# A spectral mixer with MLP: the rests' transposes in another bank pair, the last group's steps at later slots, the plain tiles' copies and stores moved, the last stores on two queues

## The chip, the cores and the metric

The kernel runs on one core of one Trainium2 chip. The metric is the device time of one execution in microseconds, from first to last instruction with what lies around it; lower is better. The core has a matrix engine (TensorE, PE in the profile, with its weight loads as PEld), a vector engine (VectorE, DVE), a scalar engine (ScalarE, ACT), a general engine (GpSimd, POOL) and an engine that only issues transfers (SyncE, SP). Each takes its own instructions strictly in program order and waits on semaphores for the others. PSUM, the memory that matmuls write, has eight banks; the large on-chip memory is SBUF.

## The reference

Four sublayers follow each other, A, B, A, B, each added to its input. x is 2048 tokens by 576 features, in fp32:

```python
def _A_ref(x, ...):            # Fourier mixing
    a = einsum("bsd,ed->bse", x, dft_hid_re)
    b = einsum("bsd,ed->bse", x, dft_hid_im)
    return einsum("ts,bse->bte", dft_seq_re, a) - einsum("ts,bse->bte", dft_seq_im, b)

def _B_ref(x, w1, b1, w2, b2): # MLP, 576 -> 4608 -> 576
    y = _layernorm(x)
    h = _gelu(einsum("bsd,df->bsf", y, w1) + b1)
    return einsum("bsf,fd->bsd", h, w2) + b2

x = x + _A_ref(_layernorm(x), ...)
x = x + _B_ref(_layernorm(x), ...)
x = x + _A_ref(_layernorm(x), ...)
x = x + _B_ref(_layernorm(x), ...)
```

## The kernel before

Every fp32 operand is split into a high and a low part (fp32r), and a product is made of three matmuls: high by high, high by low, low by high (`PASSES`). On top of it, products of 2 by 2 blocks are done with seven block products in place of eight, in the order 1, 6, 2, 5, 7, 3, 4 (`ORDER`). Sums and differences of blocks, the conversions to the high part (ScalarE) and the subtractions that give the low part (VectorE, a few on POOL) are the other engines' work. The order of all instructions is written out by hand, with Python generators that are advanced step by step; nothing is reordered afterwards.

A layer has these stages.

**Sequence** (`Sequence`, `run` at L693) multiplies by the DFT along the tokens. Two output tiles are *plain*: `first_mms` computes them with eight block products while the input is still being prepared by the steps of `fill`, tile 0 into banks 4 to 7 and then tile 1 into banks 0 to 3. `first_post` (L599) copies the four banks of one of them to a block of SBUF with four ScalarE copies, and stores the block to DRAM (`uvd`). The other 14 tiles run group by group, seven groups each: `low` (VectorE) and `high` (ScalarE) prepare the coming groups, `mms` runs 24 matmuls of one group, and `post` reads its bank. Blocks of the DFT matrix come through a ring of six (`load_c`, L622); a block goes back to the ring when `low` has used it for the last time, and the next load follows. Loads and most stores go through `dma`, which is SP's queue. `pump` advances the background work that prepares the MLP's weights.

**Hidden** (`hidden`, L869) multiplies by the DFT along the features, normalizes, and turns the tokens into the layout that the MLP wants, y, with TensorE transposes. Blocks have 288 features, two times 128 and a *rest* of 32; the rests are transposed on their own. For the last pair of tiles `turn_y` (L962) does it, in six steps: four with transposes and splits of the large parts, in bank pairs that `space` hands out, then two with the transposes and ScalarE copies of the rests (L982 to L988). The rests' transposes write the upper halves of banks 0 to 3. They are interleaved with the start of the MLP: each `next(mlp)` runs one group of seven matmuls of the first half of the tokens, whose results stand in the lower halves of the same banks.

**MLP** (`mlp`, L1061) runs on half of the tokens at a time, so four times in all. `inner(q)` (L1164) computes hidden block q, q = 0 to 17 with F = 4608, in seven groups, and leaves eight *steps* in a list: each makes one high part (ScalarE, L1235), one low part (L198, on VectorE or POOL) and perhaps a sum. `outer(g, i, side)` (L1260) multiplies two hidden blocks by the second weights, 12 matmuls per slot, two slots per i, with eight slots on one side and six on the other. `work` runs the next step of the list: once in each group of `inner`, and in two slots of three of `outer`, or in every slot from `g >= last - 1` on. An order of slots and steps that is typical: `inner(2g)`, eight slots of group g-1 (side 1), `inner(2g+1)`, six slots (side 0).

In the very first MLP the second weights are also made: `make` (L1102) returns a list of (slot number, step), and `advance` runs the steps that are due. The last group (g = 8) has a list of its own, at L1129, with its subtractions on VectorE. After a slot VectorE adds the bank to the goal (L1285, a helper at L195), and the next slot but one uses that bank again.

The final tiles are stored by `store` (L1367), in the order 4, 5, 6, 7, 0, 1, 2, 3 of the half.

`Heap` keeps the free stretches of two large SBUF tiles, and `alloc` takes the stretch that has been free the longest.

Of the kernel before, what the change touches and what calls it, by code (L numbers as in the profile page):

```python
# [8 lines left out]
F32 = mybir.dt.float32  # L9
# [148 lines left out]
def spectral_mixer(ctx: ExitStack, tc: tile.TileContext, x, dh, c0, cs, w1, b1, w2, b2, out):  # L158
# [32 lines left out]
    def dma(dst, src):  # L191
        nc.sync.dma_start(dst, src)
# [4 lines left out]
    def sub(engine, dst, a, b):  # L197
        engine.tensor_tensor(dst, a, b, op=OP.subtract)  # L198
# [122 lines left out]
    class Sequence:  # L321
# [277 lines left out]
        def first_post(self, t, out):  # L599
            uv = out(2, 2, DH)  # L600
            for i in range(2):
                for j in range(2):
                    nc.scalar.activation(uv[:, i, 1 - j], banks[4 * (1 - t) + 2 * i + j][:, :DH], AF.Copy,
                                         scale=-1.0 if i else 1.0)
            dma(uvd[t], out(2 * D))


        def load_block(self, t, k, block):
# [84 lines left out]
        def run(self, hidden):  # L693
            for p in range(NP):
                while self.ready <= p:
                    next(self.pieces)
                self.first_mms(p)

            outs = [next(b for b in self.xs if b.at != raw.at)]
            self.xs.remove(outs[0])  # L700
            self.first_post(0, outs[0])
            for _ in self.pieces:
                pass
            if outs[0].at < UV_AT + 4 * D:
                outs.pop().free()
            hidden.reserve()
            steps = self.steps
            outs.append(A.alloc(2 * D))
            self.first_post(1, outs[-1])
            for out in outs:  # L710
                clock[0] += 1
                out.free()
            for n, (t, i) in enumerate(steps):
                self.load_c()
                if n + 2 < len(steps):
                    self.low(*steps[n + 2])
                if i == 2 and t + 1 < NT:
                    self.sums(t + 1)
                self.load_c()
                if n + 3 < len(steps):  # L720
                    self.high(*steps[n + 3])
                self.mms(t, i)
                self.post(t, i)
                if t == NT - 1:
                    hidden.begin(self, ORDER.index(i))
                if n == 3 and not self.early:
                    dma(b1t, b1)
                if n % 3 == 2 and 8 <= n < 8 + 3 * KH and not self.early:
                    dma(dhd[n // 3 - 2], dh[n // 3 - 2])
                if i != 2:  # L730
                    pump()
                    pump()
            for k in range(2):
                self.L[k].free()
            self.own.close()
            for z in self.Z:
                z.free()
            hidden.take()
# [130 lines left out]
    def hidden(h, mlp):  # L869
# [92 lines left out]
        def turn_y(j):  # L962
            v = t8[j](8, DH)
            at = slice(j * P, (j + 1) * P)
            blocks = (1, 3, 2, 4, 5, 6, 7)
            for m, i0 in enumerate((2, 4, 0, 6)):
                if m % 2 == 0:
                    o = space()
                ob = o[:, m % 2]
                ni = min(2, 7 - i0)  # L970
                for i in range(ni):
                    for k in range(2):
                        nc.tensor.transpose(ob[:, (2 * i + k) * P:(2 * i + k + 1) * P],
                                            v[:, blocks[i0 + i], k * P:(k + 1) * P], ident)
                ov = ob[:, :2 * ni * P].rearrange("p (i k t) -> p i k t", k=2, t=P)
                split(y[:, i0:i0 + ni, 0:2, at], y[:, i0:i0 + ni, 3:5, at], ov)
                yield
            for i0 in (0, 4):
                ov = bank[:, i0 // 2:i0 // 2 + 2, 2 * P:].rearrange("p a (b t) -> p a b t", t=P)
                ni = min(4, 7 - i0)  # L980
                for i in range(ni):
                    nc.tensor.transpose(ov[:96, i // 2, i % 2], es(7, 96)[:, blocks[i0 + i] - 1], ident)  # L982
                for i in range(0, ni, 4 if ni == 4 else 2):
                    if ni == 4:
                        nc.scalar.activation(y[:96, 0:4, 2, at].rearrange("p (a b) t -> p a b t", a=2), ov[:96], AF.Copy)
                    else:
                        n = min(2, ni - i)
                        nc.scalar.activation(y[:96, i0 + i:i0 + i + n, 2, at], ov[:96, i // 2, :n], AF.Copy)  # L988
                yield
            t8s.give(t8.pop(j))  # L990

# [47 lines left out]
            next(mlp)  # L1039
        rests(3)  # L1040
        y_steps = turn_y(3)
        for n in (4, 1, 1):
            next(mlp)
            for m in range(n):
                if n == 4 and m == 2:
                    parts(2, slice(0, 4), slice(3, 7), high=False, engine=nc.gpsimd)
                    t8s.give(t8.pop(2))
                next(y_steps)
# [12 lines left out]
    def mlp(hid, store, first, before, after):  # L1061
# [40 lines left out]
        def make(g):  # L1102
            b11, b12, b22, b21, x = (rv[:, k] for k in range(5))
            pool = nc.gpsimd
            other = nc.vector if g == NG - 1 else pool

            def hi(i, src):
                got2[g, i] = c2.take()
                nc.scalar.activation(got2[g, i](2, 2, DH)[:, :, 0], src, AF.Copy)

            def lo(i, src):
                t = got2[g, i](2, 2, DH)
                sub(nc.vector, t[:, :, 1], src, t[:, :, 0].bitcast(F32))
                b = got2[g, i]
                soon(lambda: dma(w2s[g, i - 1], b(2, 2 * DH).bitcast(F32)))

            def soon(step):
                kept.append((at[1] + 2, step))

            one = [lambda: hi(1, b11), lambda: (lo(1, b11), sub(pool, b11, b12, b11), sub(pool, x, b22, b11))]  # L1120
            six = [lambda: hi(6, x), lambda: (lo(6, x), sub(other, x, b21, x))]
            five = [lambda: hi(5, b11), lambda: (lo(5, b11), soon(lambda: load_raw(g + 1, 0)))]
            three = [lambda: hi(3, b22), lambda: (lo(3, b22), sub(other, b12, b22, b12), soon(lambda: load_raw(g + 1, 2)))]
            seven = [lambda: hi(7, b12), lambda: (lo(7, b12), soon(lambda: load_raw(g + 1, 1)))]
            four = [lambda: hi(4, x), lambda: lo(4, x)]
            two = [lambda: hi(2, b21), lambda: (lo(2, b21), soon(lambda: load_raw(g + 1, 3)))]
            if g == NG - 1:
                return (list(zip((24, 25), one)),
                        list(zip((5, 7, 7, 8, 9, 10, 11, 12, 12, 13, 13, 14), six + five + three + seven + four + two)))  # L1129
            return (list(zip((24, 25), one)),  # L1130
                    list(zip((0, 1, 2, 3, 9, 10, 15, 16, 17, 18, 19, 20), five + six + three + seven + four + two)))

# [15 lines left out]
        def work(n):  # L1148
            for _ in range(n):
                if tasks:  # L1150
                    tasks.pop(0)()
# [12 lines left out]
        def inner(q, part=None):  # L1164
# [64 lines left out]
            def step(n):  # L1229
                if n == 0:  # L1230
                    gelu(b[3], b[3], 1)
                if n < 7:
                    k, src = parts[n]
                    H[q, k] = hs.take()
                    nc.scalar.activation(H[q, k](2, TC)[:, 0], src, AF.Copy)  # L1235
                if n:
                    k, src = parts[n - 1]
                    h = H[q, k](2, TC)
                    sub(nc.vector if n < 4 or first and q == NQ - 1 else nc.gpsimd, h[:, 1], src, h[:, 0].bitcast(F32))
                if n == 1:  # L1240
                    add(nc.vector, t, b[1], s3)
                elif n == 2:
                    sub(nc.vector, s3, b[0], s3)
                elif n == 3:
                    sub(nc.vector, s2, t, b[0])
                elif n == 4:
                    sub(nc.vector, u, b[3], s2)
                if n == 7:
                    for b_ in v:
                        tmps.give(b_)  # L1250
                    if q == NQ - 1:
                        tmps.close()
# [7 lines left out]
        def outer(g, i, side):  # L1260
            for jj in range(2):
# [11 lines left out]
                    for f in range(2):  # L1273
                        hs.give(H.pop((2 * g + f, i)))
                clock[0] += 1
                work(slot[0] % 3 < 2 or g >= last - 1)
                slot[0] += 1
                advance()
                if g == last or g == last - 1 and side == 0:
# [80 lines left out]
    for layer in range(2):  # L1360
# [3 lines left out]
        for half in range(2):  # L1364
            here = hid

            def store(j, xv):  # L1367
                t = 8 * half + j
                dma(to[t * P:(t + 1) * P, :].rearrange("p (e d) -> p e d", e=2), xv[:, :, j])

            before = after = iter(())
            if half == 0:
# [52 lines left out]
```

## Time and profile before

| | us |
|---|---|
| median of 3 runs | 2706.81 |
| the runs | 2705.21 to 2708.84 |
| profiled execution | 2707.04 |
| its span, first to last instruction | 2705.2 |
| PE busy | 2669.1 |
| VectorE busy | 1769.2 |
| ScalarE busy | 1101.6 |
| POOL busy | 794.3 |

The granted clock of TensorE was 0.999 of full speed over the span. In the profile's rows a line such as L205 is often that of a helper: L205 is every matmul, L198 every subtraction and L195 every addition on any engine, L192 every transfer on SP's queue. L1174 is a GELU, L1201 the copy of a hidden block's first group, L1235 the high part of a step, L643 the high part of a DFT block, L675 the copy of a tile's first group, L579 the high part of the four sums of an input pair. In a name such as `bank<-R` the tile written stands ahead of the tiles read: A and R are the two large SBUF tiles, bank is PSUM.

### The profile page before, as it was taken

To read this page: it belongs to the slowest core of one execution; us is meant where nothing else is said; L and a number is where in the kernel's file an instruction comes from. 1 tells how busy PE (TensorE), PEld (TensorE's weight loads), DVE (VectorE), ACT (ScalarE), POOL (GpSimd) and SP (SyncE) were. 2 spreads that over 40 slices of the span, in tenths; PEclk is the share of its full clock that TensorE was granted. 3 is DMA by queue.
4 is the path that set the end of the run, shared out by engine and by line. 5 is a ranking of instruction groups with operands and counts; after the bars stand their busy time and mean duration, and the time that the engine had idled before them with its cause. 6 is when DMAs were issued, how large, how long until landed. Compare 5 with 4: busy or idle time off the path is not lost. (4 is left out here: it accounts for less than half of the span.)

```text
span 2705.2 us, 45278 instructions
## 1 busy us (share of the span) xinstructions
PE 2669.1 (99%) x17540; PEld 2500.6 (92%) x17540; DVE 1769.2 (65%) x2573; ACT 1101.6 (41%) x1841; POOL 794.3 (29%) x740
## 2 busy tenths in 40 slices
PE   9999999999999999999999999999999999999998
PEld 9999999888888988998899999998999899898988
DVE  8888866778776565556676666466555546555555
ACT  6555544544443343333354333343333314433331
POOL 6223234544442432222250000142222234322222
PEclk9999999999999999999999999999999999999999
DMA  4777775777777466666454333546666673666664
GB/s 173 264 261 245 242 260 183 262 266 272 263 268 290 151 180 194 195 217 207 153 194 141 124 121 123 192 138 193 194 193 196 190 273 110 208 192 194 192 194 151
DMA packets 209286, 544.92 MB, mean 201 GB/s; under 512 B 22048, under 2 KB 56864, under 8 KB 208928
## 3 DMA queue, kind: packets, MB, share of 16 engines
q1 hardware_dynamic: 197408, 515.48, 58.9%
q10 hardware_dynamic: 11664, 26.55, 2.5%
q8 instruction: 139, 2.28, 0.3%
q14 instruction: 75, 0.61, 0.1%
HBM read 429.87 MB, written 114.72 MB: 201 GB/s over the span
## 5 line engine op out<-in xcount | busy, mean ns | idle before, releaser
L205 PE MATMUL bank<-R 128*128 128x288 f32 (+2 forms) x16972 | 2612.4, 315 | 17.9 <-DVE A L195 9.8
L205 PEld LDWEIGHTS bank<-R 128*128 128x128 f32 x16972 | 2438.6, 189 | 182.0 <-DVE A L195 22.4
L195 DVE TENSOR_TENSOR A<-bank,A 128x576 f32<-128x576 f32 (+3 forms) x808 | 567.9, 709 | 551.2 <-PE bank L205 471.3
L198 POOL TENSOR_TENSOR R<-A,R 128x512 fp32r<-128x512 f32 (+1 forms) x288 | 375.6, 1315 | 913.6 <-ACT R L1235 873.1
L198 DVE TENSOR_TENSOR R<-A,R 128x1024 fp32r<-128x1024 f32 (+9 forms) x521 | 494.5, 972 | 57.2 <-ACT R L643 23.6
L195 POOL TENSOR_TENSOR A<-A 128x576 f32<-128x576 f32 (+2 forms) x102 | 138.0, 1355 | 568.0 <-ACT A L683 365.4
L1174 ACT ACTIVATE bank<-bank,b1t 128x512 f32<-128x512 f32 (+1 forms) x224 | 144.9, 647 | 369.6 <-DVE bank L195 242.7
L1235 ACT ACTIVATE R<-A 128x512 fp32r<-128x512 f32 x288 | 176.0, 628 | 272.4 <-DVE A L198 118.2
L198 POOL TENSOR_TENSOR A<-A 128x384 f32<-128x384 f32 (+3 forms) x156 | 198.2, 1273 | 248.7 <-DVE R L198 128.1
L643 ACT ACTIVATE R<-A 128x1024 fp32r<-128x1024 f32 x196 | 204.6, 1052 | 120.2 <-DVE A L198 97.7
L195 DVE TENSOR_TENSOR bank<-bank,A 128x512 f32<-128x512 f32 (+1 forms) x228 | 152.2, 670 | 144.7 <-PE bank L205 143.8
L198 DVE TENSOR_TENSOR R<-bank,R 128x512 fp32r<-128x512 f32 (+1 forms) x328 | 204.9, 639 | 52.1 <-ACT R L201 46.9
L198 DVE TENSOR_TENSOR A<-A 128x1024 f32<-128x1024 f32 (+3 forms) x134 | 140.9, 1058 | 4.6 <-DVE R L198 0.4
L1201 ACT ACTIVATE A<-bank 128x512 f32<-128x512 f32 (+1 forms) x76 | 43.8, 576 | 234.9 <-PE bank L205 231.4
L1235 ACT ACTIVATE R<-bank 128x512 fp32r<-128x512 f32 x216 | 121.2, 595 | 29.8 <-PE bank L205 29.7
L198 DVE TENSOR_TENSOR A<-bank,A 128x512 f32<-128x512 f32 x144 | 97.9, 680 | 0.0
L201 ACT ACTIVATE R<-bank 128x512 fp32r<-128x512 f32 (+1 forms) x112 | 49.4, 491 | 85.3 <-PE bank L856 79.1
L1174 ACT ACTIVATE A<-bank,b1t 128x512 f32<-128x512 f32 (+1 forms) x76 | 50.6, 666 | 66.0 <-DVE bank L195 66.0
L685 DVE SCALAR_TENSOR_TENSOR A<-A 128x288 f32<-128x288 f32 x28 | 16.0, 572 | 83.3 <-POOL A L195 83.3
L275 ACT ACTIVATE R<-A 128x256 fp32r<-128x256 f32 x126 | 52.0, 413 | 44.3 <-DMA w_parts<-R 18.4
L249 ACT ACTIVATE A<-A,moments 128x576 f32<-128x576 f32 x58 | 48.6, 862 | 48.2 <-POOL moments L230 19.8
L276 ACT ACTIVATE R<-A,power,middle 128x128 fp32r<-128x128 f32 x126 | 60.8, 482 | 0.0
(67 smaller groups left out, 629.2 us busy)
## 6 DMA issues: line engine op xcount, KB each, us to landing
R<-w_parts SPq DMA_DIRECT2D x504, 320.0 KB, 3.4
R<-w_parts SPq DMA_DIRECT2D x189, 576.0 KB, 3.7
A<-in_cs SPq DMA_DIRECT2D x112, 512.0 KB, 4.1
w_parts<-R SPq DMA_DIRECT2D x63, 576.0 KB, 5.1
w_parts<-R ACTq DMA_DIRECT2D x81, 320.0 KB, 3.2
uv_mid<-A SPq DMA_DIRECT2D x32, 576.0 KB, 3.1
w_parts<-R SPq DMA_DIRECT2D x45, 320.0 KB, 4.3
A<-in_w SPq DMA_DIRECT2D x72, 192.0 KB, 4.8
```

The costliest lines, as they stand in the source:

```text
L195: engine.tensor_tensor(dst, a, b, op=op)
L198: engine.tensor_tensor(dst, a, b, op=OP.subtract)
L201: nc.scalar.activation(hi, src, AF.Copy)
L205: nc.tensor.matmul(o, a, b, start=start, stop=stop, skip_group_check=True)
L249: nc.scalar.activation(dst, src, AF.Identity, bias=mv[:, 4:5], scale=mv[:, 3:4])
L275: nc.scalar.activation(t[:, 1:4:2], src[:, 0:3:2], AF.Copy)
L276: nc.scalar.activation(t[:, 2], src[:, 1], AF.Identity, bias=power[:, 2:3], scale=middle)
L643: nc.scalar.activation(self.cells[t, i](2, NP, P)[:, 0], self.source(t, i), AF.Copy)
L685: nc.vector.scalar_tensor_tensor(uv[:, 1, 0], p7, -1.0, u, op0=OP.mult, op1=OP.subtract)
L1174: nc.scalar.activation(dst, src, AF.Gelu_apprx_tanh, bias=bias(f))
L1201: nc.scalar.activation(up, o, AF.Copy)
L1235: nc.scalar.activation(H[q, k](2, TC)[:, 0], src, AF.Copy)
```

## The change

- `turn_y`: the rests' transposes go to a bank pair from `space`, the four of the first step to its first bank, the three of the second step to its second; each step has one ScalarE copy. With (4, 0, 2) in place of (4, 1, 1) both steps come after the MLP's last group of the first token half.
- `run`: the block for the second plain tile is taken from the input ring as well, before the rest of `fill`, in place of a new `alloc` after it; its copies still follow the rest of `fill`. `hidden.reserve()` comes after both blocks are freed. `first_post` stores through ScalarE's queue.
- First MLP: the slots of the last group's list move back by up to two; in block 0, steps 4 and 5 subtract on VectorE instead of POOL.
- All MLPs: in the eight slots of group 7 (`last - 1`), side 1, a step runs in two slots of three.
- Last MLP: tiles with odd j are stored through ScalarE's queue.

```diff
-            dma(uvd[t], out(2 * D))
+            nc.scalar.dma_start(uvd[t], out(2 * D))
...
             self.first_post(0, outs[0])
+            outs.append(next(b for b in self.xs if b.at != raw.at))
+            self.xs.remove(outs[1])
             for _ in self.pieces:
                 pass
-            if outs[0].at < UV_AT + 4 * D:
-                outs.pop().free()
-            hidden.reserve()
-            steps = self.steps
-            outs.append(A.alloc(2 * D))
-            self.first_post(1, outs[-1])
+            self.first_post(1, outs[1])
             for out in outs:
                 clock[0] += 1
                 out.free()
+            hidden.reserve()
+            steps = self.steps
...
+            o = space()
             for i0 in (0, 4):
-                ov = bank[:, i0 // 2:i0 // 2 + 2, 2 * P:].rearrange("p a (b t) -> p a b t", t=P)
+                ov = o[:, i0 // 4].rearrange("p (i t) -> p i t", t=P)
                 ni = min(4, 7 - i0)
                 for i in range(ni):
-                    nc.tensor.transpose(ov[:96, i // 2, i % 2], es(7, 96)[:, blocks[i0 + i] - 1], ident)
...
+                    nc.tensor.transpose(ov[:96, i], es(7, 96)[:, blocks[i0 + i] - 1], ident)
+                nc.scalar.activation(y[:96, i0:i0 + ni, 2, at], ov[:96, :ni], AF.Copy)
                 yield
...
-        for n in (4, 1, 1):
+        for n in (4, 0, 2):
...
-                        list(zip((5, 7, 7, 8, 9, 10, 11, 12, 12, 13, 13, 14), six + five + three + seven + four + two)))
+                        list(zip((6, 8, 9, 10, 10, 11, 12, 13, 13, 14, 14, 14), six + five + three + seven + four + two)))
...
-                    sub(nc.vector if n < 4 or first and q == NQ - 1 else nc.gpsimd, h[:, 1], src, h[:, 0].bitcast(F32))
+                    sub(nc.vector if n < 4 or first and (q == NQ - 1 or q == 0 and n < 6) else nc.gpsimd, h[:, 1], src, h[:, 0].bitcast(F32))
...
-                work(slot[0] % 3 < 2 or g >= last - 1)
+                work(slot[0] % 3 < 2 or g == last - 1 and side == 0)
...
-                dma(to[t * P:(t + 1) * P, :].rearrange("p (e d) -> p e d", e=2), xv[:, :, j])
+                queue = nc.scalar if layer and half and j % 2 else nc.sync
+                queue.dma_start(to[t * P:(t + 1) * P, :].rearrange("p (e d) -> p e d", e=2), xv[:, :, j])
```

6 lines of the change are left out of this document (removed).

## The prediction

> **What bounds the kernel now.** I read the page's first lines, then the list of PE's waits, then the timeline around each wait.
>
> ```profile
> span 2705.2 us, 45278 instructions
> PE 2669.1 (99%) x17540; PEld 2500.6 (92%) x17540; DVE 1769.2 (65%) x2573; ACT 1101.6 (41%) x1841; POOL 794.3 (29%) x740
> ```
>
> ```profile
> PE bank L205 <- DVE A L195: 9.8, 7, 2.4
> PE bank L982 <- ACT A L1174: 6.5, 4, 1.6
> PE bank L982 <- ACT bank L1174: 3.6, 4, 0.9
> ```
>
> TensorE is busy 2669.1 of 2705.2 us, and the edit neither adds nor drops a matmul. What can move is therefore the waits (columns: total us, times, longest; 19.9 us in the three largest rows) and the few microseconds after the last matmul. Each part of the change is priced by the wait it touches. Everything an edit does under a PE that keeps running is worth nothing.
>
> **Part 1, the rests' transposes.** The first of four places, from the timeline (start, duration, engine, line, operation, and in brackets the idle time before it with what ended it):
>
> ```profile
> 452.80 1.08 PE L205 MATMUL bank<-R 128*128 128x256 f32 x7
> 455.00 0.42 PE L982 MATMUL bank<-ident,A 128*96 128x128 f32 x2 [0.90 <-ACT bank L1174]
> 455.52 0.60 ACT L985 ACTIVATE R<-bank 96x512 fp32r<-96x512 f32 x1 [0.57 <-PE bank L982]
> 456.91 0.75 DVE L195 TENSOR_TENSOR bank<-bank,A 128x256 f32<-128x256 f32 x2
> 457.36 0.47 ACT L1174 ACTIVATE A<-bank,b1t 128x256 f32<-128x256 f32 x1 [1.24 <-DVE bank L195]
> 457.89 0.53 PE L982 MATMUL bank<-ident,A 128*96 128x128 f32 x3 [1.63 <-ACT A L1174]
> 458.18 9.33 PE L205 MATMUL bank<-R 128*128 128x256 f32 x63
> ```
>
> The transposes write the upper halves of banks 0 to 3 while GELUs (L1174) still work on the lower halves, so they wait 0.90 and 1.63. In a pair whose readers are earlier splits, those two waits go, and PE runs group 3, group 4 and seven transposes on end. What is late next is VectorE: its add at 456.91 is in the same place of its queue, the GELU after it still ends at 457.83, and with the steps (4, 0, 2) both copies of the rests now stand behind that GELU on ScalarE. The first copy (0.60) ends near 458.4. The second half's first group needs it only in its seventh matmul. Before, that seventh began near 459.0 (458.18 and six of seven that take 1.08 together). So 0.6 us is gained, not 2.5. Bounds per place: a loss of 0.2, if all seven matmuls wait for the copy (458.4 against 458.18), and a gain of 2.5 (0.90 and 1.63). I take 0.6, worked out from the two ends of the same chain, four times: **2.4 us**.
>
> **Part 2, two subtractions from POOL to VectorE (first MLP, first block).**
>
> ```profile
> 473.92 0.69 DVE L195 TENSOR_TENSOR bank<-bank,A 128x512 f32<-128x512 f32 x1
> 474.65 4.74 PEld L205 LDWEIGHTS bank<-R 128*128 128x128 f32 x21 [0.30 <-DVE bank L195]
> 474.87 5.06 POOL L198 TENSOR_TENSOR R<-A,R 128x512 fp32r<-128x512 f32 x4
> 479.96 0.60 ACT L1201 ACTIVATE A<-bank 128x512 f32<-128x512 f32 x1 [3.54 <-POOL R L198]
> 480.61 1.66 PE L205 MATMUL bank<-R 128*128 128x512 f32 x6 [0.78 <-ACT A L1201]
> ```
>
> Four POOL subtractions (5.06 / 4 = 1.27 each) hold the copy at 479.96, and PE waits 0.78. With two of them on VectorE, POOL is done 2.5 us sooner and the 0.78 goes. But the first moved one stands ahead of VectorE's add at 473.92, whose queue has no gap there. PE's next group is already held by that add: its weights are loaded at 474.65, right at the add's end (474.61). One subtraction more (some 0.6) becomes a new PE wait of 0.6. Net **0.2 us**; bounds: 0.8 gained (the move is free) and 0.9 lost. The loss is that a moved subtraction runs beside a POOL instruction and takes as long as this one, 1.45 (three of its kind take 1.95 together in a row of part 3):
>
> ```profile
> 847.75 1.45 DVE L198 TENSOR_TENSOR R<-A,R 128x512 fp32r<-128x512 f32 x1
> 847.24 3.25 POOL L198 TENSOR_TENSOR A<-A 128x576 f32<-128x576 f32 x2 [19.76 <-DVE R L198]
> ```
>
> The Trainium skill (SBUF — State Buffer, "SBUF: two separate sides") says that a VectorE instruction with two SBUF inputs and a POOL instruction take a shared port pair exclusively, the later one blocking until the earlier is through. The row of 1.45 agrees. By that rule alone, if POOL's instruction comes first each time, the move would lose time near the lower bound above.
>
> **Part 3, the last group's steps (first MLP).** First two rows: PE's stretches around it; then VectorE's queue ahead of the long wait.
>
> ```profile
> 769.77 52.15 PE L205 MATMUL bank<-R 128*128 128x288 f32 x302
> 822.87 24.40 PE L205 MATMUL bank<-R 128*128 128x288 f32 x145 [0.94 <-DVE A L195]
> 847.89 5.05 PE L205 MATMUL bank<-R 128*128 128x288 f32 x36 [0.61 <-DVE A L195]
> 855.21 16.08 PE L205 MATMUL bank<-R 128*128 128x288 f32 x108 [2.27 <-DVE A L195]
> ```
>
> ```profile
> 851.66 1.95 DVE L198 TENSOR_TENSOR R<-A,R 128x512 fp32r<-128x512 f32 x3
> 853.64 0.76 DVE L198 TENSOR_TENSOR A<-A 128x576 f32<-128x576 f32 x1
> 854.32 0.75 DVE L195 TENSOR_TENSOR A<-bank,A 128x576 f32<-128x576 f32 x1
> ```
>
> The wait of 0.94 stands where a step runs in every slot. The stretch of 52.15 us before it holds the same place of the group before, with steps in two slots of three, and no wait that the timeline marks. Taking over that pattern gives 0.8. The two steps left over run in the next block's groups, as they do in each earlier pass. The wait of 0.61 is in the other side's slots, which keep every step: it stays. The 2.27 ends with the add at 854.32 (to 855.07), behind two subtractions of the weights' making (the last of the three in 1.95, and 853.64). With the due time moved by one slot the add follows at 852.9 and ends at 853.6; the weights' low part follows it, to 854.3, and PE's second matmul of the slot needs that. So PE goes on about 854.35: 0.9 to 1.0 gained. Later slots hold one add and one or two subtractions of 0.75 in some 1.6 us and give no new wait. Sum **1.8 us**; bounds 0 (VectorE's backlog only shifts) and 3.2 (0.94 and 2.27).
>
> **Part 4, the plain tiles.** Layer 0, then layer 1, then the loads in the page's list of DMA issues (last column: us to landing):
>
> ```profile
> 67.08 1.30 ACT L603 ACTIVATE A<-bank 128x288 f32<-128x288 f32 x4
> 68.24 1.08 ACT L643 ACTIVATE R<-A 128x1024 fp32r<-128x1024 f32 x1
> 68.82 2.50 SPq L192 DMA_DIRECT2D A<-in_cs  x3
> 69.20 0.42 ACT L675 ACTIVATE A<-bank 128x288 f32<-128x288 f32 x1
> 69.67 10.05 PE L205 MATMUL bank<-R 128*128 128x288 f32 x74 [0.43 <-ACT A L675]
> 76.85 1.23 DVE L195 TENSOR_TENSOR A<-A 128x1024 f32<-128x1024 f32 x1 [3.25 <-DMA A<-in_cs]
> 80.52 9.78 PE L205 MATMUL bank<-R 128*128 128x288 f32 x72 [0.80 <-DVE R L198]
> 80.97 0.34 ACTq L290 DMA_DIRECT2D w_parts<-R  x1
> 90.96 1.33 PE L205 MATMUL bank<-R 128*128 128x288 f32 x8 [0.65 <-DVE R L198]
> ```
>
> ```profile
> 1421.62 1.32 ACT L603 ACTIVATE A<-bank 128x288 f32<-128x288 f32 x4 [1.49 <-DVE R L198]
> ```
>
> ```profile
> A<-in_cs SPq DMA_DIRECT2D x112, 512.0 KB, 4.1
> ```
>
> The second tile's copies keep their place in ScalarE's queue; they write an older block, and their store moves from SP's queue to ScalarE's. In layer 1 the older block spares them the wait of 1.49 for a subtraction; PE has no wait there, so that is worth nothing. In layer 0 the copies have no wait to lose, and the store costs: it stands until the last copy is written (68.38), takes 0.34 to issue (as the row at 80.97), and behind it are the conversion that began at 68.24 and the copy at 69.20, for which PE waits at 69.67. Both come 0.5 later (68.38 and 0.34, against 68.24), so the 0.43 becomes 0.9: 0.5 lost. The gain is on SP, where the loads at 68.82 stood behind that store. Two of the three can go microseconds sooner. The third, issued last (about 71.0, 0.3 before the row's end) and still waiting for VectorE, then finds no transfer ahead of it. It was waited for until 76.85, 5.8 us; at the usual 4.1 it comes 1.7 sooner. So do the two sums and the subtraction that end at 80.5, and the 0.80 goes. The chain behind 90.96 starts with those sums: its 0.65 goes too. In layer 1 the same load ends a wait of 0.1. Sum: 0.80 + 0.65 + 0.1 - 0.5, **1.1 us**. Bounds: 2.0 gained (the 0.43 goes as well, the issue being hidden) and 0.5 lost (the loads land no sooner, because the transfers before them and not the order of issue make them slow).
>
> **Part 5, the last stores on two queues.** Their issues in the timeline, and a stretch of six microseconds (busy time of PE, weight loads, VectorE, ScalarE, POOL; clock; DMA share, GB/s):
>
> ```profile
> 2696.09 5.49 SPq L192 DMA_DIRECT2D out<-A  x8
> 2697.50:2703.50 6.00, 1.02 (x8) 0.79 (x6) 0.99 (x2) 0.00 (x0) 0.15 (x1) 0.93 1.08 381
> ```
>
> SP takes 5.49 us to issue eight stores, so halving that seems worth up to 2.7 us. But in the 6 us after the first packets the sixteen DMA engines are busy all the time (share 1.08, 381 GB/s), and the eight 288 KB stores are what they carry. I take **0**; bounds: 2.7 gained, 0.5 lost (one issue more on ScalarE's sequencer). The Trainium skill (DMA: Bandwidth & Descriptors, "Issuing engines are not separate DMA queues") states that several issuing engines save only issue time, since all run on the same sixteen engines; the share of 1.08 agrees, and by that rule this part is worth at most the issue time.
>
> **The sum.** 2.4 + 0.2 + 1.8 + 1.1 + 0 = 5.5 us off. The profiled execution took 2707.04 us (its span of 2705.2 and 1.8 around it), 0.2 above the median of 2706.81. So 2701.5 for such an execution, and **2701.3** for the median. What a measurement tells from no change is about 0.2%, that is 5.4 us: the line is at 2701.4, and the forecast lies on it.
>
> **The rivals.** *The waits only move*: the seven matmuls behind the rests all wait for the copy (0.2 lost four times) and VectorE's backlog in the last group gives back half of its 1.8. Then 5.5 - 3.2 - 0.9 = 1.4 us stay: 2705.4, no change that counts. For it speaks that VectorE, not the bank, ends each of these chains; against it that each matmul waits for its own operands, as six of the seven need no rest. *The chain behind the GELU opens too*, because the two splits of VectorE ahead of its add come sooner: 2.5 per place, 13.1 us in all, 2693.7. Nothing in the diff moves those splits. *Slower*: the blocks the plain tiles now take change which hole every later tile's output gets; if that is the block whose store still runs, the copy into it waits for the landing. There are 14 such tiles in each layer:
>
> ```profile
> uv_mid<-A SPq DMA_DIRECT2D x32, 576.0 KB, 3.1
> ```
>
> The next tile's first copy comes about two groups after a store's issue (3.3 each, so 6.6), and a store lands in 3.1. It begins to cost once landing takes over 6.6; with 5.5 gained it makes the kernel slower from 6.8 on, and past the line of 0.2% from 7.0. At 7.2, 28 times 0.6 is 16.8 us, less 5.5: 2718.1. Landing times would have to double.
>
> **How the numbers follow.** Chances: forecast 0.56, waits only move 0.28, chain opens 0.07, slower 0.09. The line divides the forecast's own share, with 0.3 of it past the line; of the second case a few hundredths lie past it, and of the last a little stays within: faster 0.41, same 0.51, slower 0.08. Range 2697.9 to 2705.6: below, the forecast with 0.85 more at each of the four places of part 1 (towards its bound of 2.5 in place of 0.6); above, the second case. The upper bounds of parts 1 and 5 and the third rival lie outside, with the chances they have.
>
> **What would show it.** After: no wait at the rests' transposes, one of about 2 us inside the second half's first group instead; no wait near 480.6, one of 0.6 near 475; about 0.1 where 0.94 was and 1.3 where 2.27 was, 0.61 unchanged; 0.9 near 69.67, none near 80.5 and 91; landings of the last stores as before. Wrong if a rests' wait shrinks by far more or not at all, if ScalarE's store makes PE wait longer than 1 us near 70, or if the last stores end much sooner after the last matmul.

## The result and the profile after

| us | before | after |
|---|---|---|
| median of the runs shown together (7 each) | 2708.84 | 2699.63 |
| lowest to highest | 2705.21 to 2711.87 | 2696.92 to 2701.74 |
| profiled execution | 2707.04 | 2698.2 |
| its span | 2705.2 | 2696.4 |

The ratio is 0.9969 (95% interval 0.9959 to 0.9979): 0.31% faster, which is more than the 0.2% that a measurement tells from no change. The forecast was 2701.3, just past that line. The time lies inside the range, 1.7 us below the forecast, and in the case that had got a chance of 0.41 (faster), not in the one that had got 0.51 (same). That it came so near is in part luck. The forecast took 5.5 us off a median of 2706.81, from three runs; in the larger set before's median is 2708.84, and the gain is 9.2 us by the medians and 8.4 by the ratio. The base was 2.0 us too low and the gain about 3 too small.

Busy times from the page, and the largest of PE's waits, after:

```profile
PE 2665.2 (99%) x17540; PEld 2502.2 (93%) x17540; DVE 1771.5 (66%) x2575; ACT 1101.1 (41%) x1837; POOL 789.5 (29%) x738
```

```profile
PE bank L205 <- ACT R L983: 8.7, 4, 2.2
PE bank L205 <- DVE A L195: 7.7, 7, 2.4
```

The two rows of the rests' transposes (L982, 6.5 and 3.6) are gone. A new row stands first: four waits of up to 2.2 us for the ScalarE copies of the rests (L983). PE's busy time fell by 3.9 us, although its matmuls are as many as before (17540). Busy time that shrinks with the same matmuls was time in which matmuls took longer than they need, and the list of waits doesn't hold it.

To see where the time went I compared the start of the same matmul, counted along PE's queue, in both profiled executions. Negative is earlier after the change:

| place (us in before) | what lies there | gain or loss | forecast |
|---|---|---|---|
| 60 to 95 | plain tiles, layer 0 | -1.51 | -0.95 |
| 445 to 466 | rests, place 1 | -0.57 by the wait, +1.49 by the clock | -0.6 |
| 466 to 490 | block 0, the two subtractions | -0.31 | -0.2 |
| 815 to 830 | first MLP, the steps | -0.98 | -0.8 |
| 830 to 870 | first MLP, the due times | -2.07: about -1.0 by the wait, -1.4 by the clock, +0.4 given back | -1.0 |
| 945 to 966 | rests, place 2 | -0.49 | -0.6 |
| 1310, 2165, 2648 | last group of the other three MLPs | -0.56, -0.57, -0.51 | 0 |
| 1345 to 1360 | start of layer 1 | -0.87 | 0 |
| 1430 to 1450 | plain tiles, layer 1 | -0.41 | -0.1 |
| 1790 to 1816 | rests, place 3 | -0.78 | -0.6 |
| 2275 to 2299 | rests, place 4 | +1.01: about -0.5 by the wait, +1.5 by the clock | -0.6 |
| all the rest | hundredths at a time inside the MLPs | -1.69 | 0 |
| last matmul | the sum | -8.82 | -5.5 |

**The rests.** The timeline after at the first place (start, duration, engine, line, in brackets the idle time before and what ended it):

```profile
452.89 0.93 PE L982 MATMUL bank<-ident,A 128*96 128x128 f32 x7
453.57 0.96 PE L205 MATMUL bank<-R 128*128 128x256 f32 x6
455.25 0.75 DVE L195 TENSOR_TENSOR bank<-bank,A 128x256 f32<-128x256 f32 x2
455.70 0.47 ACT L1169 ACTIVATE A<-bank,b1t 128x256 f32<-128x256 f32 x1 [2.42 <-DVE bank L195]
456.07 0.96 ACT L983 ACTIVATE R<-bank 96x512 fp32r<-96x512 f32 x2
456.71 6.55 PE L205 MATMUL bank<-R 96*128 96x256 f32 x40 [2.18 <-ACT R L983]
```

PE runs the seven transposes on end and six matmuls of the next group. Then the seventh waits 2.18 us for the rest's copy, which stands behind the GELU at 455.70, which waits for VectorE's add at 455.25. This is the row the prediction announced: one wait of about 2 us inside the second half's first group.

**The clock.** Stretches of 3.4 us (busy time of PE, weight loads, VectorE, ScalarE, POOL; then the granted clock), first of before, then after the rests' wait at the four places:

```profile
856.10:859.50 3.40, 3.40 (x17) 3.40 (x16) 2.08 (x4) 0.00 (x0) 0.00 (x0) 0.50 1.04 425
```

```profile
458.20:461.60 3.40, 3.40 (x18) 3.40 (x17) 0.69 (x2) 1.04 (x2) 0.00 (x0) 0.50 0.82 264
956.10:959.50 3.40, 3.40 (x31) 3.40 (x30) 1.29 (x3) 1.00 (x3) 0.00 (x0) 1.00 0.81 264
1806.20:1809.60 3.40, 3.40 (x30) 3.40 (x30) 1.29 (x3) 1.05 (x3) 0.00 (x0) 1.00 0.91 320
2287.80:2291.20 3.40, 3.40 (x19) 3.40 (x18) 0.42 (x1) 0.65 (x2) 0.00 (x0) 0.50 0.56 169
```

At places 1 and 4 PE is "busy" for all 3.40 us but begins 18 or 19 matmuls where 30 or 31 begin at places 2 and 3: the granted clock is 0.50. Such a stretch costs some 1.5 us, more than the whole gain at the place. Before the change the same happened once, at 856.1, after the wait of 2.27. After it that wait is short, and the stretch is gone:

```profile
846.28 5.03 PE L205 MATMUL bank<-R 128*128 128x288 f32 x36 [0.58 <-DVE A L195]
852.14 0.37 PE L205 MATMUL bank<-R 128*128 128x288 f32 x1 [0.83 <-DVE A L195]
852.71 14.90 PE L205 MATMUL bank<-R 128*128 128x288 f32 x107 [0.21 <-DVE R L198]
```

The Trainium skill (TensorE: Matmul & The Clock Gate, "What's actually happening") says that the gate passes either four or eight of eight pulses, decided by how busy the array was in a free-running window of 3.4 us. The rows agree: 0.50 or 1.00, for 3.4 us (6.8 in some runs below). Its rule of thumb ("HAM oscillation — how this bites in real kernels") asks for no idle gap above about 3.4 us. Here the measurement differs: a wait of 2.18 was enough at places 1 and 4, and the same wait was not at places 2 and 3. A free-running window would do that, and the traces show where its edges lie. Within each execution the half-clock stretches start whole multiples of 3.413 us apart, to 0.004 us (eight of the ten profiled executions have more than one). So every execution can be cut into windows at these edges. The window ahead of the half clock at place 1, and the one at place 2 that holds most of the wait, after:

```profile
454.81:458.22 3.41, 1.51 (x12) 1.52 (x13) 1.37 (x5) 1.71 (x4) 0.85 (x1) 1.00 0.76 207
953.15:956.56 3.41, 2.25 (x18) 2.25 (x19) 0.88 (x3) 1.86 (x5) 0.11 (x1) 1.00 0.24 61
```

At place 1 PE is idle for 1.90 us of the window, at place 4 for 2.18, and the half clock begins where the window ends. At places 2 and 3 an edge cuts the wait in two, and no window is idle for more than 1.29. I counted the windows of all ten profiled executions, between 100 and 2640 us, that ran at the full clock. PE was idle for 1.81 us or more in 14 of them, and a half clock followed all 14. It followed one of the three with 1.72, 1.73 and 1.80, and none of the 7396 with 1.69 or less. By this count the idle time within one window decides, and not the length of a wait. In before a longer wait, 2.41 at 1342.35, was cut by an edge into 0.86 and 1.55 and drew no half clock.

**The other three MLPs.** Here PE's list of waits has nothing in either kernel. PE's weight loads and the chain of work show it, before:

```profile
1309.32 1.62 PEld L205 LDWEIGHTS bank<-R 128*128 128x128 f32 x12 [0.26 <-DVE A L195]
1311.18 1.66 PEld L205 LDWEIGHTS bank<-R 128*128 128x128 f32 x12 [0.24 <-DVE A L195]
```

```profile
2646.36 1.85 PE bank L205 x12
```

nine slots on end (108 matmuls) in the last group of all, before:

```profile
2683.82 14.44 PE L205 MATMUL bank<-R 128*128 128x288 f32 x108
```

and the weight loads of the same slots after the change, where one such wait is left of three:

```profile
1304.48 15.62 PEld L205 LDWEIGHTS bank<-R 128*128 128x128 f32 x94 [0.26 <-DVE A L195]
```

Before, three slots on end begin with a weight load that waits a quarter of a microsecond for VectorE's add. The matmul ahead is still draining meanwhile, so PE counts as busy, yet such a slot takes 1.85 us. In the undisturbed stretch it is 1.60 (14.44 / 9).

**The plain tiles**, after, where the second tile's copies and store stand in ScalarE's queue:

```profile
67.11 1.29 ACT L603 ACTIVATE A<-bank 128x288 f32<-128x288 f32 x4
68.43 0.33 ACTq L605 DMA_DIRECT2D uv_mid<-A  x1
68.80 1.06 ACT L643 ACTIVATE R<-A 128x1024 fp32r<-128x1024 f32 x1 [0.40 <-ACT A L603]
69.76 0.39 ACT L675 ACTIVATE A<-bank 128x288 f32<-128x288 f32 x1
70.21 10.97 PE L205 MATMUL bank<-R 128*128 128x288 f32 x81 [0.89 <-ACT A L675]
74.68 1.22 DVE L195 TENSOR_TENSOR A<-A 128x1024 f32<-128x1024 f32 x1 [1.06 <-issue]
```

The sum that waited for a load until 76.85 before begins at 74.68 and waits for no DMA. The two loads that went out at 68.82 and 69.30 before are now issued at 36.36 and 42.68, and the third, at 71.06, lands in 3.5 us instead of 5.8. The waits at 80.5 and 91 are gone; the one at 69.67 went from 0.43 to 0.89.

**The last stores**, after: the issues, and six microseconds at the same distance from the last matmul as the stretch shown of before:

```profile
2687.28 3.85 SPq L1365 DMA_DIRECT2D out<-A  x4
2687.28 3.96 ACTq L1365 DMA_DIRECT2D out<-A  x4
```

```profile
2688.68:2694.68 6.00, 1.02 (x8) 0.79 (x6) 0.99 (x2) 0.00 (x0) 0.16 (x1) 0.94 1.07 379
```

Issuing is over 1.5 us after the last matmul instead of 3.1, but the DMA engines are as full as before (1.07, 379 GB/s), and from the last matmul's end to the end of the span it is 6.70 us against 6.73.

### The profile page after: what moved, and what is told of

The parts are those of the page before. It is cut to its first block, busy times and chain, and to the rows that moved or that the text cites. A ratio compares the mean times of both kernels' runs of the same rounds, so it can differ in the third digit from the quotient of the medians.

```text
span 2696.4 us, 45272 instructions
## 1 busy us (share of the span) xinstructions
PE 2665.2 (99%) x17540; PEld 2502.2 (93%) x17540; DVE 1771.5 (66%) x2575; ACT 1101.1 (41%) x1837; POOL 789.5 (29%) x738
```

## The experiments

Each kernel was timed beside the kernel before, in three sets: the change; rests_only to copies_first; due_only to loads_first, on another chip. The medians of before were 2708.84, 2708.92 and 2709.02. A difference between medians of two sets is less sure than a ratio within one. The fourth column is the mean granted clock of the single runs.

| run | median us | ratio to before | clock |
|---|---|---|---|
| the change | 2699.63 | 0.9969 (0.9959 to 0.9979) | .997 to .999 |
| rests_only | 2705.79 | 0.9990 (0.9981 to 0.9999) | .996 to .999 |
| steps_only | 2705.32 | 0.9986 (0.9977 to 0.9995) | .995 to .998 |
| fill | 2696.67 | 0.9955 (0.9941 to 0.9968) | .998 to .999 |
| copies_first | 2692.91 | 0.9939 (0.9927 to 0.9952) | .998 to .999 |
| due_only | 2705.23 | 0.9993 (0.9983 to 1.0002) | .996 to 1.0 |
| plain_only | 2707.47 | 0.9997 (0.9988 to 1.0006) | .995 to .999 |
| store_on_sp | 2701.62 | 0.9972 (0.9961 to 0.9983) | .997 to .999 |
| loads_first | 2691.91 | 0.9942 (0.9929 to 0.9954) | .998 to .999 |

The single parts are small against the scatter of the runs, so their profiles, matmul by matmul, decide more than their medians. The four single parts (rests_only, steps_only, due_only, plain_only) add up to 0.34% by their ratios, against 0.31% for the change. The two subtractions of part 2 and the stores of part 5 had no run of their own.

### rests_only: the rests' transposes alone

```diff
-                ov = bank[:, i0 // 2:i0 // 2 + 2, 2 * P:].rearrange("p a (b t) -> p a b t", t=P)
+                ov = o[:, i0 // 4].rearrange("p (i t) -> p i t", t=P)
...
-        for n in (4, 1, 1):
+        for n in (4, 0, 2):
```

Expected:

> Only the rests' part of the change, on the kernel before. Clock theory: the two waits of 0.9 and 1.63 us become one of about 2.2 us, each place gains 0.5 to 0.6 us, but a wait over 2 us can be followed by 3.4 us at half the granted clock, which costs about 1.5 us. With two such stretches in the four places the part gains 2.2 - 3.0, so it is worth between 2.2 us faster and 1 us slower, and the granted clock over the run does not rise. Rival (the half-clock stretches have nothing to do with PE's waits): 2.0 to 2.4 us faster, and no more half-clock stretches than in the kernel before.

Measured: 2705.79; the ratio is 0.10% below 1 (0.01% to 0.19%), some 2.7 us. By place the same matmul comes 0.48 earlier, 0.96 later, 0.77 earlier and 0.47 earlier. The one loss is the clock, after a wait of 2.18 at 956.63; here it is place 2, which ran at 1.00 in the full change:

```profile
956.50:959.90 3.40, 3.27 (x15) 3.27 (x16) 0.42 (x1) 0.84 (x3) 0.00 (x0) 0.51 0.45 107
1338.80:1345.60 6.80, 4.80 (x21) 4.45 (x20) 4.73 (x6) 2.08 (x3) 2.06 (x2) 0.50 0.36 129
```

So the wait itself is worth about half a microsecond a place, as forecast. Which of the waits above 2 us draws a half clock differs from one execution to the next: here one also stands at 1338.8, where the change touches nothing, and none at 855, where the wait of 2.27 is still present. In this execution an edge at 854.14 cuts that wait into 1.01 and 1.26.

The two shorter waits of the old order can draw a half clock too, where enough of them falls into one window: in plain_only at places 2 and 3 (1.72 and 1.85 idle), in steps_only at place 3 (1.81). Over the profiled executions that is 3 of 16 places with the two waits (before, steps_only, due_only, plain_only), and 4 of 12 with the single wait of 2.18 (the change, rests_only, store_on_sp).

### steps_only: a step in two slots of three in the last group

```diff
-                work(slot[0] % 3 < 2 or g >= last - 1)
+                work(slot[0] % 3 < 2 or g == last - 1 and side == 0)
```

Expected:

> Only the change of work() in outer, on the kernel before: on side 1 of group 7 a step in two slots of three. First MLP: the 0.94 us wait near 823 falls to about 0.1. The other three MLPs show no PE wait there, so by the list of PE's waits they give nothing, 0.9 us in all. Rival from the two traces: in the kernel before each slot there begins with a weight load that waits about 0.25 us, which delays PE by 0.17 to 0.19 us although PE shows almost no idle time; three times 0.55 us more, so 2.5 us in all.

Measured: 2705.32, and by matmul -1.0 near 823, then -0.58, -0.55 and -0.55 in the last groups of the other MLPs. All four gain. The two slots near 2646 that took 1.85 us each in the chain of work are now inside one piece:

```profile
2644.16 16.03 PE bank L205 x94
```

VectorE's part in it is seen in its busy time over those two slots (third of the busy times) in before, and in its add for the slot after them in steps_only:

```profile
2646.36:2650.06 3.70, 3.69 (x24) 3.23 (x24) 3.70 (x7) 1.15 (x2) 1.58 (x2) 1.00 0.56 184
```

```profile
2649.22 0.76 DVE L195 TENSOR_TENSOR A<-bank,A 128x576 f32<-128x576 f32 x1 [0.56 <-PE bank L205]
```

With a step in every slot VectorE had no gap at all. Two subtractions and an add took it 1.86 us (adds at 2647.42 and 2649.28), and PE's slot came to 1.85, with the quarter microsecond that the weight loads show. In steps_only VectorE is as full over these two slots (3.69 of 3.70), but the next slot brings no step, and ahead of its add VectorE waits 0.56 for PE: it has caught up. The reading that the condition matters in the first MLP alone falls.

### fill: matmuls in place of a part of the wait

The change, with the first matmul of the second half's first group issued nine more times. The extra ones start the same sum anew, so they only fill time.

```diff
                 for n, (l, r) in enumerate(todo):
+                    if q == 0 and part == 1 and i == 1 and n == 0:
+                        for _ in range(9):
+                            mm(o, l, r, True, False)
```

Expected:

> The changed kernel with the first matmul of the second half's first group issued nine more times (the group starts over with the tenth, so the result is the same): about 1.2 us of the 2.2 us wait behind the rests' copy is filled with work that nobody needs. Clock theory: all four waits fall to about 1 us, no half-clock stretch follows one, the mean granted clock rises, and the kernel is up to 3 us faster than the changed one although it does more work. Rival (half-clock stretches by chance): the number of such stretches stays, time as the changed kernel, within 0.5 us.

Measured: 2696.67, 3.0 us below the change itself, with 36 matmuls more. At the first place:

```profile
453.69 2.04 PE L205 MATMUL bank<-R 128*128 128x256 f32 x15
456.84 5.42 PE L205 MATMUL bank<-R 96*128 96x256 f32 x43 [1.12 <-ACT R L983]
```

```profile
457.00:460.40 3.40, 3.40 (x29) 3.40 (x30) 0.85 (x2) 1.59 (x4) 0.00 (x0) 1.00 0.69 222
```

The seventh matmul starts when it did (456.84 against 456.71), since the copy hasn't moved; only the idle time ahead of it is 1.12 instead of 2.18. At all four places the clock stays at 1.00 afterwards, and the profiled execution has no half clock before its end. The span is 3.4 us shorter than the change's (2693.0 against 2696.4), and the two half clocks that are gone account for 3.0 of it. So work that nobody needs made the kernel faster, and the idle time costs beyond its length. The medians alone would not settle it: they come from two sets, the single runs overlap by 0.9 us (highest 2697.84 here, lowest 2696.92 there), and so do the intervals of the ratios.

### copies_first: the rests' steps ahead of the last group

The change with (4, 2, 0): both steps of the rests, and so their ScalarE copies, come before the last group of the first half and its GELU.

```diff
-        for n in (4, 0, 2):
+        for n in (4, 2, 0):
```

Expected:

> The changed kernel with the steps of the last pair as (4, 2, 0): both of the rests' copies come before the GELU of the last group on ScalarE instead of behind it. If what sets the remaining wait is ScalarE's order (the copies behind a GELU that waits for VectorE's add), the wait of 2.2 us goes, PE runs the first two groups of the second half while VectorE catches up, and each of four places gains about 1.2 us more, 5 us in all and up to 3 us from the clock. Rival (VectorE's splits set the wait wherever the copies stand): no more than 1 us gained, the wait only moves to the third group.

Measured: 2692.91 (2692.53 to 2693.41), 6.7 us below the change. The first place:

```profile
452.48 1.04 PE L982 MATMUL bank<-ident,A 128*96 128x128 f32 x7 [0.35 <-DVE R L198]
453.12 0.98 ACT L983 ACTIVATE R<-bank 96x512 fp32r<-96x512 f32 x2
453.27 2.75 PE L205 MATMUL bank<-R 128*128 128x256 f32 x21
455.60 0.47 ACT L1169 ACTIVATE A<-bank,b1t 128x256 f32<-128x256 f32 x1 [1.50 <-DVE bank L195]
456.40 6.78 PE L205 MATMUL bank<-R 128*128 128x256 f32 x45 [0.39 <-ACT A L1196]
```

The GELU still waits for VectorE and starts at the same time as in the change (455.60 against 455.70). But the copies are done at 454.1, in time in which ScalarE is idle in the change (2.42 ahead of the GELU at 455.70), and PE runs 21 matmuls on end. Idle time at the place is 0.74 in place of 2.18. The late copy was a matter of ScalarE's order. By matmul the four places are 2.7, 1.2, 1.2 and 2.7 us ahead of the change: 1.2 each by the wait, as expected, and 1.5 more at the two that had a half clock. Some 2 us of it are lost again near 1330, to the one half clock left before the end, in a part that no version touches. It follows a wait of 2.02 that ends at 1328.76, and a wait of 1.35 lies inside it:

```profile
1329.20:1336.00 6.80, 5.45 (x23) 5.10 (x22) 5.05 (x7) 1.26 (x3) 1.31 (x1) 0.50 0.48 161
```

### due_only: the due times alone

```diff
-                        list(zip((5, 7, 7, 8, 9, 10, 11, 12, 12, 13, 13, 14), six + five + three + seven + four + two)))
+                        list(zip((6, 8, 9, 10, 10, 11, 12, 13, 13, 14, 14, 14), six + five + three + seven + four + two)))
```

Expected:

> Only the last group's due times, on the kernel before. If the slot behind the last making steps waits for VectorE's add alone, the wait of 2.27 us near 855 falls to about 1.3 and PE is 0.95 us ahead; and as 1.3 us is well under two, no half-clock stretch follows it, which in the profiled execution of before cost about 1.4 us more: 1 to 2.4 us faster. Rival (VectorE's backlog only shifts to later slots): the wait shrinks, but new ones of together about 1 us open in the next eight slots, 0 us.

Measured: 2705.23; the interval of the ratio takes in 1. In the profile the wait of 2.27 is 0.83 and 0.20, and the clock behind it stays up:

```profile
854.01 0.37 PE L205 MATMUL bank<-R 128*128 128x288 f32 x1 [0.83 <-DVE A L195]
```

```profile
854.30:857.70 3.40, 3.20 (x24) 3.12 (x24) 2.99 (x5) 0.00 (x0) 0.00 (x0) 1.00 1.07 416
```

By matmul this is some 2.4 us earlier at 864, of which 1.0 is the wait and 1.4 the half clock that before's execution had here; 0.3 is given back by 870.

### plain_only: the plain tiles alone

```diff
-            dma(uvd[t], out(2 * D))
+            nc.scalar.dma_start(uvd[t], out(2 * D))
...
+            outs.append(next(b for b in self.xs if b.at != raw.at))
+            self.xs.remove(outs[1])
```

Expected:

> Only the plain tiles' part (older block, store on ScalarE's queue), on the kernel before. As in the trace of the changed kernel: the wait at 69.67 grows from 0.43 to 0.9, those at 80.5 and 91 go, and PE is 1.4 to 1.6 us ahead by 100 us; in layer 1 0.3 to 0.4 us ahead near 1440; 1.9 us in all. Rival (the forecast's working): 0.5 lost, 1.45 gained, 0.1 in layer 1, so 1.1 us.

Measured: 2707.47, not told apart from before. The profile shows the part clearly: +0.48 at 70, -1.07 at 80, -0.92 at 91, so 1.5 us by 95, and 0.40 near 1440.

```profile
70.00 25.25 PE L205 MATMUL bank<-R 128*128 128x288 f32 x189 [0.91 <-ACT A L675]
```

The execution had four stretches of half clock (at 854, 957, 1339 and 1810), which hide these 1.9 us in the total.

### store_on_sp: the change with the plain tiles' stores back on SP's queue

```diff
-            nc.scalar.dma_start(uvd[t], out(2 * D))
+            dma(uvd[t], out(2 * D))
```

Expected:

> The changed kernel with the plain tiles' stores back on SP's queue (the older block stays). If the order on SP's queue makes the loads late: the wait near 70 falls back to 0.4, those near 80 and 90 come back with 0.8 and 0.65, and the kernel is 1.0 to 1.5 us slower than the changed one. Rival (the transfers ahead and not the order of issue make the loads slow, or the older block is what helped): no wait comes back, and the kernel is 0.5 us faster than the changed one.

Measured: 2701.62. In the profile, against the change, -0.50 at 70, +0.91 at 80 and +0.92 at 91, so 1.3 us later by 95, as expected:

```profile
68.35 0.33 SPq L192 DMA_DIRECT2D uv_mid<-A  x1
68.77 2.50 SPq L192 DMA_DIRECT2D A<-in_cs  x3
...
76.64 1.23 DVE L195 TENSOR_TENSOR A<-A 128x1024 f32<-128x1024 f32 x1 [3.10 <-DMA A<-in_cs]
...
80.32 0.93 PE L205 MATMUL bank<-R 128*128 128x288 f32 x5 [0.64 <-DVE R L198]
```

Three loads go out together at 68.77, right behind the store, and VectorE waits for them as in before. Blocks and copies are those of the change, so the store's place in SP's queue alone brings and takes the waits at 80 and 91.

### loads_first: the loads ahead of the store, on SP's queue

copies_first with the store on SP's queue, and the loads of the DFT blocks issued before the second plain tile's copies and store.

```diff
-            nc.scalar.dma_start(uvd[t], out(2 * D))
+            dma(uvd[t], out(2 * D))
...
+            self.load_c()
             self.first_post(1, outs[1])
```

Expected:

> The changed kernel with the steps (4, 2, 0) and with the two loads issued on SP's queue ahead of the second plain tile's store, which is back on SP's queue. If it is the order on SP's queue, the loads are as early as in the changed kernel and ScalarE is free of the issue: the waits near 80 and 90 stay away, the one near 70 is 0.4 and not 0.9, and the kernel is 0.5 us faster than with the steps (4, 2, 0) alone (2692.9), so near 2692.4. Rival (the store on another queue than the loads is what helps): the waits near 80 and 90 come back, 1 us slower, near 2694.

Measured: 2691.91 (2691.68 to 2693.04), the fastest of all, 7.7 us below the change and 17 below before:

```profile
61.01 1.33 SPq L192 DMA_DIRECT2D A<-in_cs  x2
68.82 0.33 SPq L192 DMA_DIRECT2D uv_mid<-A  x1
70.09 11.11 PE L205 MATMUL bank<-R 128*128 128x288 f32 x82 [0.45 <-ACT A L675]
```

Two loads now go out at 61.01, 7.8 us sooner than in before, and the second tile's store stands behind them instead of ahead. That is later than in the change (36.36 and 42.68), since the first tile's store still precedes them, and yet soon enough. ScalarE issues nothing here, so the wait near 70 is 0.45 again, and those at 80 and 91 stay away. Against copies_first this is 0.5 us in the profile; the medians are 1.0 apart, from two sets, with runs that overlap.

## Why the prediction was right or wrong

**Part 1, the rests: the wait right, the clock left out.** The wait that remains, its length, the GELU it stands behind and the matmul it holds are those forecast, and the waits' gain of 0.57, 0.49, 0.78 and 0.5 is what 0.6 a place stood for. What failed is that "So 0.6 us is gained" counts a wait of 2.18 as 2.18. Before the change the idle time was in two pieces, 0.90 and 1.63, with 1.3 us of work between them; after it, it is one piece, and in two of four places a half clock follows that costs 1.5. In this one execution part 1 is a loss of 0.7 instead of a gain of 2.4. That isn't its mean: the single wait drew a half clock at 4 of 12 places, the two waits of before at 3 of 16, and rests_only is some 2.7 us faster by its ratio. The argument was already in the profile of before: a wait of 2.27 at 855.21, and 0.50 behind it.

**Part 2: right.** The 0.78 goes, a wait of 0.55 comes at 474.58 (0.6 at 475 was said), net 0.31 against 0.2. The price of a shared port, which was the lower bound, didn't come due: the moved subtraction at 474.44 took 0.71 beside POOL's, not 1.45. POOL's two that remained took 1.5 each (3.01 together) instead of 1.27, and PE didn't wait for them.

**Part 3: the largest part, and under-sized.** In the first MLP it was right by step: 0.94 to nothing the list shows, 0.61 unchanged (0.58), 2.27 to 1.04 in two pieces where 1.3 was said, 0.8 and 1.0 gained. Two things were missed. The other three MLPs were priced at nothing, by the prediction's rule that an edit under a PE that keeps running is worth nothing, because PE's list of waits shows none there. The list doesn't show a wait that lies in the weight load while the last matmul drains. That is 1.6 us. And the half clock behind the 2.27 went with it, 1.4 us. Forecast 1.8, found 4.7.

**Part 4: right by mechanism, a little small.** The store on ScalarE costs 0.47 (0.5 said), and the loads behind SP's queue are what the store held up, as store_on_sp shows. The mis-sized terms are the two waits that go: listed at 0.80 and 0.65, they gave 1.08 and 0.91, a quarter microsecond more each. The weight loads at the head of these stretches stood idle for 1.03 and 0.88 in before, near what was gained. That would be the same quarter microsecond that the slots of the other MLPs lose without a listed wait; it is argued from these rows, and no run tells it apart. Near 1440 the gain was 0.41 where 0.1 was said.

**Part 5: right.** Nothing (6.73 to 6.70). The Trainium skill (DMA: Bandwidth & Descriptors, "Issuing engines are not separate DMA queues") agrees: the two queues share the same sixteen engines, and only issuing became shorter.

**The sum.** -5.5 was said and -8.8 was found in the profiled pair: part 1 is 3.1 worse, parts 2 to 4 are 3.8 better, and 2.6 lie elsewhere: 0.87 at the start of layer 1, where a wait of 1.13 for a subtraction is nearly gone, and 1.69 in hundredths of a microsecond inside the MLPs. Of the 1.69, 0.91 lie between 2305 and 2640. There rests_only, steps_only, due_only and plain_only, which edit nothing that runs there, are also 1.01, 0.83, 0.84 and 0.43 ahead of before, so most of this belongs to before's execution and not to the change. For the rest no cause was found. The wait at the start of layer 1 is 0.8 to 1.1 in the profiles of steps_only, due_only and copies_first, and gone in plain_only and store_on_sp. The plain tiles' part could have removed it, but copies_first has that part too.

**The rivals.** "The waits only move" fell, since each place gave its 0.6. "The chain behind the GELU opens too" did not come from the change, as forecast, but its price was real: copies_first collects 1.2 of its 1.9 us per place without any split coming sooner, by passing the copies ahead of the GELU. "Slower, by a hole of the heap" has no wait in the profile to show for it.

What stays open: where the edges of the clock's window will fall in a coming execution, so which wait of 2 us will cost; how much of the difference between the medians is the half clocks. The kernel before itself took 2705.2 and 2705.76 at a mean clock of 1.0 and 2713.24 and 2713.68 at 0.994, among the 21 runs beside the first experiments, so most of the scatter goes with the clock.

## What to carry to other kernels

A wait of the matrix engine can cost more than its length once it is near 2 us, or once several short ones add up to that within 3.4 us: look at the granted clock in the microseconds behind each of the longest waits, and split or fill such a wait even where the chain that sets it can't be shortened. Look for lost time in the weight loads and in what a slot takes, not only in PE's list of waits. And before moving an instruction to other memory, ask which in-order queue it stands in and what stands behind it: here the order of two steps gave more than the new banks, and two loads issued ahead of a store gave what a second queue did, without its price.

## What the hardware showed unexpectedly

- The granted clock changes at the edges of windows of 3.413 us that run on through the whole execution. In ten profiled executions a half clock followed all 14 full-clock windows in which PE was idle for 1.81 us or more, and none with 1.69 or less. It lasted 3.4 or 6.8 us; a stretch of 3.4 us costs 1.4 to 1.5 us.
- So the same wait of 2.18 drew a half clock at two of four places of one execution, a wait of 2.41 cut by an edge drew none, and waits of 1.12 drew none at four of four.
- A weight load that waits 0.25 us at the head of a slot makes the slot 0.25 us longer (1.85 against 1.60) while PE shows no idle time that the list counts.
- Spreading the issue of eight stores over two queues ended issuing 1.5 us sooner after the last matmul, and their landing not at all.
